# First spectral stage fed with x transposed: mean as a row, rstd behind the product, no transposes

## The chip, the core and the metric

The kernel runs on one core of a Trainium2 chip. The metric is device microseconds of one execution. Three runs of the kernel before gave 1438.41, 1438.85 and 1439.46 us, a median of 1438.85 us.

## The reference

The input x has 2048 rows (positions) of 576 features. Every row is normalised by its mean and variance, and the result goes two ways that are added to x: a filter in the two-dimensional frequency domain, and a gated unit with 4608 hidden features.

```
xn = layernorm(x)                                  # per row of 576, no weights
A  = irfft2(rfft2(xn) * (w_r + 1j * w_i))          # over 2048 x 576
B  = (sigmoid(xn @ w_gate) * (xn @ w_up)) @ w_down # 576 -> 4608 -> 576
out = x + A + B
```

All data are float32.

## The kernel before

Products run on TensorE (PE) in a rounded 32-bit form, and nearly every product is made three times with split operands: a rounded high part (made by ScalarE, ACT) and the rest as a low part (made by VectorE, DVE, as a subtraction). So a value that TensorE is to read passes ACT and then DVE.

The gated unit is the bulk: the rows go in two halves of 1024, and for each half a loop over 36 blocks of 128 hidden features (`unit`) makes seven products (`made(0)` to `made(6)`) of seven matmuls of 512 columns each (tiles `pA`, `pB`, `pE`). In the first half, the weights of a block are split and written to DRAM (`wsp`), and in the second half they come back from there, slice by slice, in one buffer (`w`). After each product of the second half one item of the down projection follows (`seven`, tiles `ps`, six matmuls of 288 columns), whose sums DVE adds to `qs` and `acc`.

The spectral filter runs beside the second half's units, a little after each product, in steps: `active` holds generators, and each `yield` in one is a step, which is one product of seven matmuls and one `ps` item. It has three phases: phase1b (16 tiles of 128 rows, each started 4.1 steps after the last), phase2 and phase3. Phase1b, with rows of 576 features stored as 288 and their mirror image, does for each tile `t`:

- load the rows (`xb`) in natural layout, wait four steps, normalise them (`norm`, line 383), add and subtract the mirrored halves (`eo`, line 468), split the last 32 columns (`rp`, lines 204, 205 and 472);
- two steps later, turn the tile by six transposes on PE (`pf`, lines 478 and 479), and split the result out of PSUM into `fh`, `fl` and `fr` (lines 204, 205 and 484);
- two steps later, multiply by the cosine and sine tables: 14 matmuls into `pd` (line 494). Out of `pd` come four pieces of 64 partitions, each as a high part `ah` by ACT and a low part `al` by DVE (lines 204 and 205, inside `split`);
- two steps later, six matmuls into `pa` (line 506) with a table `am`, whose result goes to DRAM (`sc1`) for phase2.

The mean `mv` and reciprocal deviation `rstd` of the second half's rows are made in the first half by `later_stats`, one tile of rows every fourth unit.

The tiles `ps`, `pf`, `pd` and `pa` all come from one PSUM pool with two slots (`pair`). The order on an engine is not the program's alone: the layer that builds the program moves instructions of one engine past each other where it expects a wait, except those marked `keep_in_program_order`. Each engine then runs its own list in order. DMAs of phase1b are issued from the SP queue, which is in order as well.

Of the kernel before, what the change touches and what calls it, by code (L numbers as in the profile page):

```python
# [9 lines left out]
F32 = mybir.dt.float32  # L10
F32R = mybir.dt.float32r
I32 = mybir.dt.int32
AF = mybir.ActivationFunctionType
OP = mybir.AluOpType
PSUM = bass.MemoryType.PSUM

P = 128
S, D, F = 2048, 576, 4608
KD = D // 2 + 1
NQ = KD + 1  # L20
N1, N2 = 64, 32
NT = S // P
EPS = 1e-5
HD = D // 2
FR = HD + 1 - 2 * P
CW = 512
TPC = CW // P
PAIRS = S // (2 * CW)
TPP = 2 * TPC
KT = 2  # L30
REM = HD - KT * P
# [6 lines left out]
KR = 3 * REM  # L38
# [84 lines left out]
COLS = np.concatenate([np.arange(HD), np.arange(HD, D)[::-1]])  # L123
ROWS = np.arange(S).reshape(N1, N2).T.ravel()


def _layout(x, w_r, w_i, w_gate, w_up, w_down):

    ks = np.concatenate([np.arange(KT * P), np.tile(np.arange(KT * P, HD), 4)])
    w = np.stack([w_gate[COLS], w_up[COLS]]).reshape(2, 2, HD, NF, P)[:, :, ks]  # L130
    w = w[[1, 1, 0, 0], [0, 1, 1, 0]].reshape(4, KT + 1, P, NF, P).transpose(3, 2, 0, 1, 4)
    v = np.stack([w_r, w_i])[:, :, KOF].reshape(2, N1, N2 // 2, 2, KD).transpose(2, 1, 0, 3, 4)
    v = np.broadcast_to(v[:, None], (N2 // 2, 2, N1, 2, 2, KD))
    lay = {"x": x.reshape(S, D)[ROWS][:, COLS].reshape(NT, P, D), "ri": v.reshape(N2 // 2, P, 4 * KD),
           "w": w.reshape(NF, P, 4 * (KT + 1) * P), "wd": w_down[:, COLS].reshape(NF, P, D)}
    return {k: np.ascontiguousarray(a) for k, a in lay.items()}

# [5 lines left out]


@with_exitstack
def spectral_glu_kernel(ctx: ExitStack, tc: tile.TileContext, x, ri, w_in, w_down, out):
    nc = tc.nc
    con = {k: nc.inline_tensor(v, name=f"c_{k}").ap() for k, v in _constants().items()}

    def f32(ap):  # L150
        return ap.bitcast(F32)

    def load_r(dst, src):
        nc.sync.dma_start(f32(dst), src)
# [3 lines left out]
    def pair(name):  # L158
        return ps.tile([P, 2, 512], F32, tag="pp", name=name, bufs=2)

    fix = ctx.enter_context(tc.tile_pool(name="fix", bufs=1))
    idf = fix.tile([P, P], F32, name="idf")
    idr = fix.tile([P, P], F32R, name="idr")
    mv = fix.tile([P, NT, 2], F32, name="mv")
    rstd = fix.tile([P, NT], F32, name="rstd")
# [12 lines left out]
    acc = {}  # L178


    sc1 = tc.dram_tile([N2 * P, NQ], F32, name="sc1")
    sc2 = tc.dram_tile([N2 * P, NQ], F32, name="sc2")
    spill = tc.dram_tile([TPP * P, D], F32, name="spill")
# [19 lines left out]
    def split(hi, lo, src, eng=None):  # L203
        nc.scalar.activation(hi, src, AF.Copy)
        (eng or nc.vector).tensor_tensor(lo, src, f32(hi), op=OP.subtract)


    R = {}
# [134 lines left out]
    def load_x(dst, t):  # L343
        nc.sync.dma_start(dst, x[t])
# [7 lines left out]
    def moments(src, t, pool):  # L352
        st = pool.tile([P, 2, 6], F32, tag="st", name=f"st{t}", bufs=2)
        for i in range(2):
            placed(nc.vector.bn_stats(st[:, i, :], src[:, i * HD:(i + 1) * HD]))
        nc.vector.bn_aggr(mv[:, t, :], st.rearrange("p a b -> p (a b)"))

    def scales(t0, n, pool, table):
        ts = slice(t0, t0 + n)
        rs = pool.tile([P, 4, n], F32, tag="rs", name=f"rs{t0}", bufs=2)  # L360
        ve, r0, w0, w1 = (rs[:, i] for i in range(4))
        nc.vector.tensor_scalar(ve, mv[:, ts, 1], EPS, None, op0=OP.add)
        if table:
            nc.scalar.activation(w0, ve, AF.Sqrt)
            nc.vector.reciprocal(r0, w0)
            steps = 1
        else:

            nc.vector.tensor_scalar(w1.bitcast(I32), ve.bitcast(I32), 1, None, op0=OP.logical_shift_right)
            nc.vector.tensor_scalar(r0.bitcast(I32), w1.bitcast(I32), -1.0, float(0x5F3759DF), op0=OP.mult, op1=OP.add)  # L370
            steps = 3
        nc.vector.tensor_scalar(ve, ve, -0.5, None, op0=OP.mult)
        for k in range(steps):
            nc.vector.tensor_tensor(w0, r0, r0, op=OP.mult)
            nc.vector.tensor_tensor(w0, w0, ve, op=OP.mult)
            o = rstd[:, ts] if k == steps - 1 else r0
            nc.vector.scalar_tensor_tensor(o, w0, 1.5, r0, op0=OP.add, op1=OP.mult)
        nc.vector.scalar_tensor_tensor(nmr[:, ts], mv[:, ts, 0], -1.0, rstd[:, ts], op0=OP.mult, op1=OP.mult)

    def norm(o, a, t):  # L380

        tc.keep_in_program_order(
            nc.vector.tensor_scalar(o, a, mv[:, t, 0:1], rstd[:, t:t + 1], op0=OP.subtract, op1=OP.mult))

    XS, XR, RM = {}, {}, {}

    def new_xs(p, m):
# [64 lines left out]

    def phase1b(t):
        pool, cf = R["pool"], R["cf"]
        xb = pool.tile([P, D], F32, tag="xb", name=f"xb{t}", bufs=2)
        load_x(xb, t)
        yield
        yield  # L460
        yield
        yield
        norm(xb, xb, t)
        am = pool.tile([P, 2, 2, P], F32R, tag="am", name=f"am{t}", bufs=2)
        load_r(am, con["am"][:, t * 4 * P:(t + 1) * 4 * P].rearrange("p (a h m) -> p a h m", a=2, h=2))
        eo = pool.tile([P, 2, HD], F32, tag="eo", name=f"eo{t}")
        for e, op in ((0, OP.add), (1, OP.subtract)):
            nc.vector.tensor_tensor(eo[:, e], xb[:, :HD], xb[:, HD:], op=op)
        rp = pool.tile([P, 2, 3, REM], F32R, tag="rp", name=f"rp{t}")
        rem = eo[:, :, 2 * P:]  # L470
        split(rp[:, :, 0, :], rp[:, :, 1, :], rem)
        nc.scalar.activation(rp[:, :, 2, :], rem, AF.Copy)
        yield
        yield
        pt = pair(f"pf{t}")
        for e in range(2):
            for k in range(2):
                nc.tensor.transpose(pt[:, 0, (2 * e + k) * P:(2 * e + k + 1) * P], eo[:, e, k * P:(k + 1) * P], idf)  # L478
            nc.tensor.transpose(pt[:KR, 1, e * P:(e + 1) * P].bitcast(F32R), rp[:, e].rearrange("p a b -> p (a b)"), idr)
        fh = pool.tile([P, 2, 2, P], F32R, tag="fh", name=f"fh{t}")  # L480
        fl = pool.tile([P, 2, 2, P], F32R, tag="fl", name=f"fl{t}")
        fr = pool.tile([P, 2, P], F32R, tag="fr", name=f"fr{t}")
        split(fh, fl, pt[:, 0, :].rearrange("p (e k s) -> p e k s", e=2, k=2))
        nc.scalar.activation(fr[:KR], pt[:KR, 1, :2 * P].rearrange("p (e s) -> p e s", e=2), AF.Copy)
        yield
        yield
        pd = pair(f"pd{t}")
        for e in range(2):
            steps = []
            for k in range(2):  # L490
                steps += [(fh[:, e, k, :], cf[:, e, k, :]), (fl[:, e, k, :], cf[:, e, k, :]), (fh[:, e, k, :], cf[:, e, 2 + k, :])]
            steps.append((fr[:KR, e, :], cf[:KR, e, 4, :]))
            for n, (l, r) in enumerate(steps):
                nc.tensor.matmul(pd[:, e, :NQ], l, r, start=n == 0, stop=n == len(steps) - 1)  # L494
        ah = pool.tile([P, 2, NQ], F32R, tag="ah", name=f"ah{t}", bufs=1)
        al = pool.tile([P, 2, NQ], F32R, tag="al", name=f"al{t}", bufs=1)
        for sl in range(2):
            for ci in range(2):
                o = slice(ci * N1, (ci + 1) * N1)
                split(ah[o, sl, :], al[o, sl, :], pd[sl * N1:(sl + 1) * N1, ci, :NQ])  # L500
        yield
        yield
        pa = pair(f"pa{t}")
        for sl in range(2):
            for n, (h, m) in enumerate(((0, ah), (0, al), (1, ah))):
                nc.tensor.matmul(pa[:, sl, :NQ], am[:, sl, h, :], m[:, sl, :], start=n == 0, stop=n == 2)  # L506
        x1 = pool.tile([P, 2, NQ], F32, tag="x1", name=f"x1{t}", bufs=1)
        nc.scalar.activation(x1, pa[:, :, :NQ], AF.Copy)
        nc.sync.dma_start(sc1[2 * t * P:(2 * t + 2) * P].rearrange("(j p) n -> p j n", j=2), x1)
# [422 lines left out]
    def later_stats(t):  # L932
        xt = R["pool"].tile([P, 5, HD], F32, tag="xa", name=f"xt{t}", bufs=TPC)
        xt = xt.rearrange("p a d -> p (a d)")[:, :D]
        load_x(xt, t)
        for _ in range(4):
            yield
        moments(xt, t, R["pool"])
        if t == NT - 1:
            scales(TPP, TPP, R["pool"], False)  # L940

    def blocks(p, c):
        for mm in range(2):
# [76 lines left out]
    for p in range(PAIRS):  # L1020
# [38 lines left out]
        for f in range(G, NF):  # L1059
# [16 lines left out]
            if p == 0 and f and f % 4 == 0:  # L1076
                sides.append(later_stats(TPP + f // 4 - 1))
# [62 lines left out]
```

## Time and profile before

| what | value |
|---|---|
| median of three runs | 1438.85 us |
| the profiled execution, whole | 1438.32 us |
| its span, first to last instruction | 1436.5 us |
| PE busy | 1422.8 us (99%) |
| DVE busy | 1087.7 us (76%) |
| ACT busy | 653.5 us (45%) |
| DMA queue q1, share of 16 engines | 69.8% |
| phase1b in the span | from about 736 us (first `pf`) to 954 us (last `pa`) |

The span is the time between the first and the last instruction; the whole execution has 1.8 us more around it. PE is nearly always busy by the profile, but matmuls overlap in flight, so the busy time and the single durations of PE say less than the distance from one piece of work to the next. The chain of waits (the page's part 4) gives that distance.

### The profile page before, as it was taken

Reading aid. Unit: us, or ns where it says so; the run is one execution under the profiler, and the core shown is the slowest. Engines: PE = TensorE matmul, PEld = TensorE weight load, DVE = VectorE, ACT = ScalarE, POOL = GpSimd, SP = SyncE. Lnnn points to the kernel's source line nnn. Section 1 sums busy time; section 2 is a strip of 40 time slices with the busy share of each in tenths; the row PEclk is TensorE's granted clock in tenths of the full one; section 3 lists DMA queues with packets and bytes.
Section 4 is the critical chain, followed back from the end, with each engine's and each line's share of the span. In section 5 each row is a group of like instructions: output and inputs, shape, how many; then the busy total and the mean of one; then the engine's idle time right before and its main releaser. Section 6 shows DMA issues by size and latency. Waiting matters only on the chain.

```text
span 1436.5 us, 21196 instructions
## 1 busy us (share of the span) xinstructions
PE 1422.8 (99%) x8073; PEld 1252.0 (87%) x8073; DVE 1087.7 (76%) x1734; ACT 653.5 (45%) x1122; POOL 3.3 (0%) x5
## 2 busy tenths in 40 slices
PE   8999999999999999999999999999999999999998
PEld 5888888888888888889888888888888889898997
DVE  7988888888888787766366687767888877766784
ACT  6644444444444444453345454434555534443431
POOL 0000000000000000000000000000000000000000
PEclk9999999999999999999999999999999999999999
DMA  7588677776777776655676766778888787776642
GB/s 247 195 329 313 256 274 264 265 264 255 262 255 271 262 276 232 230 215 181 213 215 204 210 201 207 206 220 269 273 270 269 245 282 243 226 227 195 202 125 83
DMA packets 128325, 338.79 MB, mean 236 GB/s; under 512 B 11872, under 2 KB 49248, under 8 KB 123360
## 3 DMA queue, kind: packets, MB, share of 16 engines
q1 hardware_dynamic: 127296, 336.13, 69.8%
q8 instruction: 64, 1.05, 0.3%
q10 hardware_dynamic: 928, 1.31, 0.2%
q14 instruction: 37, 0.30, 0.1%
HBM read 201.27 MB, written 136.12 MB: 235 GB/s over the span
## 4 chain that ended last, share of the span: by engine, by line
PE 97%; DVE 1%; ACT 1%; issue 0%; DMA 0%; ACTq 0%
PE pB L644 24%; PE po L751 19%; PE pE L644 16%; PE pA L644 16%; PE ps L842 12%; PE pe L602 2%; PE pd L494 2%; PE pc L546 1%; PE pa L506 1%; PE pb L530 1%; PE py L573 1%; PE pf L478 1%; PE pz L585 1%; PE b L900 0%; PE px_S L442 0%; PE px_A L442 0%
## 5 line engine op out<-in xcount | busy, mean ns | idle before, releaser
L644 PE MATMUL pB<-X,w 128*128 128x512 f32 x1484 | 382.4, 394 | 0.0
L644 PEld LDWEIGHTS pB<-X,w 128*128 128x128 f32 x1484 | 267.5, 188 | 49.5 <-ACT v L708 1.3
L644 PE MATMUL pE<-X,w 128*128 128x512 f32 x1064 | 273.1, 393 | 0.0
L644 PE MATMUL pA<-X,w 128*128 128x512 f32 x1008 | 259.7, 394 | 1.9 <-DVE X L448 1.2
L644 PEld LDWEIGHTS pE<-X,w 128*128 128x128 f32 x1064 | 192.8, 188 | 34.0
L644 PEld LDWEIGHTS pA<-X,w 128*128 128x128 f32 x1008 | 184.2, 189 | 35.8 <-DVE X L448 1.9
L751 PE MATMUL po<-wd,hh 128*128 128x288 f32 x1216 | 210.9, 295 | 0.0
L842 PEld LDWEIGHTS ps<-wf,hs 128*128 128x128 f32 x1260 | 188.6, 188 | 19.3 <-DVE qs L852 1.8
L842 PE MATMUL ps<-wf,hs 128*128 128x288 f32 x1260 | 204.2, 296 | 0.3 <-DVE qs L852 0.3
L751 PEld LDWEIGHTS po<-wd,hh 128*128 128x128 f32 x1216 | 184.4, 188 | 11.2
L755 DVE TENSOR_TENSOR acc<-acc,po 128x576 f32<-128x576 f32 x168 | 126.0, 750 | 76.7 <-PE po L751 75.5
L236 ACT ACTIVATE w<-raw 128x768 fp32r<-128x768 f32 (+1 forms) x106 | 100.8, 952 | 94.2 <-PE pE L644 37.9
L751 PE MATMUL po<-wd,hl 128*128 128x288 f32 x608 | 128.9, 293 | 0.0
L852 DVE TENSOR_TENSOR qs<-qs,ps 128x576 f32<-128x576 f32 x112 | 84.1, 751 | 31.1 <-PE ps L842 30.0
L751 PEld LDWEIGHTS po<-wd,hl 128*128 128x128 f32 x608 | 98.7, 189 | 0.0
L852 DVE TENSOR_TENSOR acc<-acc,ps 128x576 f32<-128x576 f32 x90 | 67.5, 750 | 24.2 <-PE ps L842 23.6
L238 DVE TENSOR_TENSOR w<-raw,w 128x512 fp32r<-128x512 f32 (+1 forms) x106 | 81.9, 773 | 3.2 <-ACT w L236 2.9
L729 DVE TENSOR_TENSOR y<-y,g 128x1024 f32<-128x1024 f32 x67 | 81.9, 1222 | 3.2
L709 DVE TENSOR_TENSOR y<-v,pE 128x512 f32<-128x512 f32 x68 | 46.7, 686 | 49.1 <-ACT v L708 48.2
L778 ACT ACTIVATE hs<-y 128x512 fp32r<-128x512 f32 x105 | 64.9, 629 | 38.9 <-DVE y L729 12.4
L712 ACT ACTIVATE g<-pB 128x512 f32<-128x512 f32 x68 | 40.7, 598 | 91.1 <-PE pB L644 91.1
L708 ACT ACTIVATE v<-pB 128x512 f32<-128x512 f32 x68 | 40.7, 598 | 71.9 <-PE pB L644 71.5
(165 smaller groups left out, 1667.9 us busy)
## 6 DMA issues: line engine op xcount, KB each, us to landing
w<-wsp SPq DMA_DIRECT2D x246, 320.0 KB, 3.5
wsp<-w SPq DMA_DIRECT2D x34, 2240.0 KB, 7.8
raw<-in_w SPq DMA_DIRECT2D x34, 768.0 KB, 9.7
wdsp<-wd SPq DMA_DIRECT2D x36, 576.0 KB, 4.6
wf<-tsp SPq DMA_DIRECT2D x60, 288.0 KB, 3.8
wf<-wdsp SPq DMA_DIRECT2D x45, 288.0 KB, 4.0
std<-in_wd SPq DMA_DIRECT2D x36, 288.0 KB, 5.4
ri<-in_ri SPq DMA_DIRECT2D x16, 578.0 KB, 5.3
```

The costliest lines, as they stand in the source:

```text
L236: placed(nc.scalar.activation(o[:, :, :3, :], src, AF.Copy))
L238: placed(nc.vector.tensor_tensor(o[:, :, 3:, :], src[:, :, :KT, :], f32(o[:, :, :KT, :]), op=OP.subtract))
L644: nc.tensor.matmul(bank, w[:, sw, :], X[:, x, sx, :], start=start and j == 0, stop=stop and j == len(STEPS) - 1, skip_group_check=skip)
L708: nc.scalar.activation(v[:, 1], bank["B"], AF.Copy)
L709: nc.vector.tensor_tensor(y[:, 1], v[:, 1], bank["E"], op=OP.add)
L712: nc.scalar.activation(g[:, 1], bank["B"], AF.Sigmoid)
L729: nc.vector.tensor_tensor(y, y, g, op=OP.mult)
L751: nc.tensor.matmul(pd[:, b, :HD], h[i], w[k][b], start=g == 0 and n == 0, stop=g == G - 1 and n == 2)
L755: nc.vector.tensor_tensor(a, a, pd[:, :, :HD], op=OP.add)
L778: nc.scalar.activation(hs[:, 0], src, AF.Copy)
L842: nc.tensor.matmul(pd[:, i, :HD], h[:, a, m], w[:, b], start=q == 0, stop=q == 2)
L852: nc.vector.tensor_tensor(o, o, pd[:, :, :HD], op=OP.add)
```

## The change

The rows for phase1b are handed over a second time, as a second input `xt`, already transposed: partitions are features, columns are the tile's 128 rows, and both mirrored halves stand side by side. The 32 remaining features of a half are written four times over, so that a third block of 128 partitions holds their copies. Everything between the load and `pd` then works in that layout, and PE makes no `pf`.

The mean is no longer a value per partition but a row. Subtracting the halves cancels it, so only the sum needs it, as twice the mean, from a tile `mb` on which the row of means has been spread over the partitions by a DMA. The rows come from two new transposes (`prow`) at the end of `later_stats`, through a DRAM tile `rowd`. The factor `rstd` is applied behind the product, where rows are partitions again: ACT scales by it as it makes `ah`, and DVE's subtraction for `al` becomes a three-operand instruction that multiplies by it first. The number of matmuls in `pd` and `pa` stays. The two steps between `eo` and `pf` fall away, and the load of `am` is issued at the tile's start instead of four steps later.

```diff
 def phase1b(t):
-        xb = pool.tile([P, D], F32, tag="xb", name=f"xb{t}", bufs=2)
-        load_x(xb, t)
+        xs = pool.tile([P, 2, KT + 1, P], F32, tag="xs", name=f"xs{t}", bufs=2)
+        nc.sync.dma_start(xs.rearrange("p h k s -> p (h k s)"), xt[t])
+        mb = pool.tile([P, P], F32, tag="mb", name=f"mb{t}", bufs=2)
+        nc.sync.dma_start(mb, rowd[0, t].partition_broadcast(P))
+        am = pool.tile([P, 2, 2, P], F32R, tag="am", name=f"am{t}", bufs=2)
+        load_r(am, con["am"][...])
         yield   # four times
-        norm(xb, xb, t)
-        am = pool.tile(...); load_r(am, con["am"][...])
-        eo = pool.tile([P, 2, HD], F32, tag="eo", name=f"eo{t}")
-        for e, op in ((0, OP.add), (1, OP.subtract)):
-            nc.vector.tensor_tensor(eo[:, e], xb[:, :HD], xb[:, HD:], op=op)
-        rp = pool.tile([P, 2, 3, REM], F32R, tag="rp", name=f"rp{t}")
-        rem = eo[:, :, 2 * P:]
-        split(rp[:, :, 0, :], rp[:, :, 1, :], rem)
-        nc.scalar.activation(rp[:, :, 2, :], rem, AF.Copy)
-        yield
-        yield
-        pt = pair(f"pf{t}")
-        for e in range(2):
-            for k in range(2):
-                nc.tensor.transpose(pt[:, 0, ...], eo[:, e, k * P:(k + 1) * P], idf)
-            nc.tensor.transpose(pt[:KR, 1, ...].bitcast(F32R), rp[:, e]..., idr)
-        split(fh, fl, pt[:, 0, :].rearrange("p (e k s) -> p e k s", e=2, k=2))
-        nc.scalar.activation(fr[:KR], pt[:KR, 1, :2 * P]..., AF.Copy)
+        eo = pool.tile([P, 2, KT + 1, P], F32, tag="eo", name=f"eo{t}")
+        tc.keep_in_program_order(nc.vector.tensor_tensor(eo[:, 1], xs[:, 0], xs[:, 1], op=OP.subtract))
+        nc.vector.scalar_tensor_tensor(xs[:, 0], mb.unsqueeze(1).to_broadcast([P, KT + 1, P]), -2.0, xs[:, 0], op0=OP.mult, op1=OP.add)
+        nc.vector.tensor_tensor(eo[:, 0], xs[:, 0], xs[:, 1], op=OP.add)
+        nc.scalar.activation(fh, eo, AF.Copy)
+        nc.vector.tensor_tensor(fl, eo[:, :, :KT], f32(fh[:, :, :KT]), op=OP.subtract)
+        r = slice(REM, 2 * REM)
+        nc.vector.tensor_tensor(fh[r, :, KT], eo[r, :, KT], f32(fh[r, :, KT]), op=OP.subtract)
         yield
         yield
...
-                split(ah[o, sl, :], al[o, sl, :], pd[sl * N1:(sl + 1) * N1, ci, :NQ])
+                v, r = pd[i, ci, :NQ], rstd[i, t:t + 1]
+                nc.scalar.activation(ah[o, sl, :], v, AF.Copy, scale=r)
+                nc.vector.scalar_tensor_tensor(al[o, sl, :], v, r, f32(ah[o, sl, :]), op0=OP.mult, op1=OP.subtract)
...
 # later_stats, behind the last tile's scales:
+            yield
+            pr = pair("prow")
+            rows = R["pool"].tile([NT, 2, P], F32, tag="xa", name="rows", bufs=TPC)
+            for i, v in enumerate((mv[:, :, 0], rstd)):
+                nc.tensor.transpose(pr[:NT, i, :P], v, idf)
+            nc.scalar.activation(rows, pr[:NT, :, :P], AF.Copy)
+            nc.sync.dma_start(rowd.rearrange("i t p -> t i p"), rows)
```

Since nine lines come in ahead of it and some go, line 494 (`pd`) of before is 482 in the changed kernel, 506 (`pa`) is 497, 644 is 635 and 842 is 833.

The order moves with it, and only between 736 us and the end of phase1b; elsewhere it differs by the two `prow` alone. On PE, the second tile of phase1b stood so before, from its transposes to the first of its `pd`:

```order
L644 MATMUL pB_6649<-X,w_6208 128x512 x4
L478 MATMUL pf_6813<-idf,eo_6753 128x128 x2
L644 MATMUL pB_6649<-X,w_6208 128x512 x2
L842 MATMUL ps_2_1_6834<-wf_2_6668,hs_2_6721 128x288
L479 MATMUL pf_6813<-idr,rp_6756 96x128
L478 MATMUL pf_6813<-idf,eo_6753 128x128 x2
L479 MATMUL pf_6813<-idr,rp_6756 96x128
L842 MATMUL ps_2_1_6834<-wf_2_6668,hs_2_6721 128x288 x5
L644 MATMUL pE_6650<-X,w_6208 128x512 x7
L842 MATMUL ps_3_0_6851<-wf_3_6719,hs_3_6799 128x288 x6
L494 MATMUL pd_6865<-cf,fh_6820 128x290
L494 MATMUL pd_6865<-cf,fl_6821 128x290
```

The same place on PE in the changed kernel, up to the first `pd` that reads the low part:

```order
L635 MATMUL pB_6663<-X,w_6215 128x512 x7
L833 MATMUL ps_2_0_6803<-wf_2_6682,hs_2_6747 128x288 x6
L482 MATMUL pd_6817<-cf,fh_6765 128x290
L635 MATMUL pB_6663<-X,w_6215 128x512 x3
L482 MATMUL pd_6817<-cf,fl_6766 128x290
```

The transposes are gone, `pd` stands about two steps earlier, and three matmuls of `pB` have been moved in between its first matmul (which reads `fh`) and its second (which reads `fl`). Ten of the 16 tiles have such a piece of 2 to 4 matmuls there; before, none had.

On PE again, from the last `pd` of the third tile to its first `pa`, before:

```order
L494 MATMUL pd_7012<-cf,fr_6968 128x290
L644 MATMUL pB_6906<-X,w_6208 128x512 x7
L842 MATMUL ps_5_1_7058<-wf_5_6858,hs_5_6945 128x288 x6
L644 MATMUL pB_6906<-X,w_6208 128x512 x7
L842 MATMUL ps_6_0_7076<-wf_6_6942,hs_6_7008 128x288 x6
L506 MATMUL pa_7089<-ah_7027,am_6891 128x290
```

And in the changed kernel:

```order
L482 MATMUL pd_6953<-cf,fh_6895 128x290 x2
L635 MATMUL pB_6910<-X,w_6215 128x512 x7
L833 MATMUL ps_4_1_6986<-wf_4_6810,hs_4_6877 128x288 x6
L635 MATMUL pA_6909<-X,w_6215 128x512 x7
L833 MATMUL ps_5_0_7004<-wf_5_6874,hs_5_6949 128x288 x6
L635 MATMUL pB_6910<-X,w_6215 128x512 x4
L497 MATMUL pa_7018<-ah_6968,am_6774 128x290
```

The work between `pd` and the `pa` that needs its split result has grown by four matmuls of 512 columns. Over all 16 tiles there stand 12 `ps` matmuls in between, before and after, and beside them before 15, 15, 14, 15, 15, 14, 14, 17, 14, 15, 14, 14, 14, 19, 14, 12 matmuls of 512 columns (235 in all), and now 20, 15, 18, 15, 15, 13, 16, 20, 17, 12, 17, 17, 15, 17, 20, 16 (263).

On DVE, the third tile's preparation stood so before:

```order
L383 TENSOR_SCALAR xb_6760<-xb_6760,mv,rstd 128x576
L468 TENSOR_TENSOR eo_6893<-xb_6760 128x288 x2
L205 TENSOR_TENSOR rp_6896<-eo_6893,rp_6896 128x2x32
L205 TENSOR_TENSOR fl_6967<-pf_6959,fh_6966 128x512
L205 TENSOR_TENSOR al_7028<-pd_7012,ah_7027 64x290 x2
```

And in the changed kernel, where `L843` is the addition of a `ps` item and the `al` are the second tile's:

```order
L464 TENSOR_TENSOR eo_6891<-xs_6770 128x384
L465 SCALAR_TENSOR_TENSOR xs_6770<-mb_6772,xs_6770 128x384
L491 SCALAR_TENSOR_TENSOR al_6833<-pd_6817,rstd,ah_6832 64x290
L466 TENSOR_TENSOR eo_6891<-xs_6770 128x384
L843 TENSOR_TENSOR acc<-acc,ps_2_1_6850 128x2x288
L491 SCALAR_TENSOR_TENSOR al_6833<-pd_6817,rstd,ah_6832 64x290
L470 TENSOR_TENSOR fl_6896<-eo_6891,fh_6895 128x512
L472 TENSOR_TENSOR fh_6895<-eo_6891,fh_6895 32x2x128
L491 SCALAR_TENSOR_TENSOR al_6833<-pd_6817,rstd,ah_6832 64x290
```

One tile's preparation now lies between another tile's `al`, where before the two followed each other.

More of the change, by code (lines that the diff above doesn't have):

```diff
@@ L133, in _layout @@
     v = np.broadcast_to(v[:, None], (N2 // 2, 2, N1, 2, 2, KD))
-    lay = {"x": x.reshape(S, D)[ROWS][:, COLS].reshape(NT, P, D), "ri": v.reshape(N2 // 2, P, 4 * KD),
+    x = x.reshape(S, D)[ROWS][:, COLS]
+    xt = x.reshape(NT, P, 2, HD)[..., ks].reshape(NT, P, 2, KT + 1, P).transpose(0, 4, 2, 3, 1)
+    lay = {"x": x.reshape(NT, P, D), "xt": xt.reshape(NT, P, 2 * (KT + 1) * P), "ri": v.reshape(N2 // 2, P, 4 * KD),
            "w": w.reshape(NF, P, 4 * (KT + 1) * P), "wd": w_down[:, COLS].reshape(NF, P, D)}
@@ L145, in spectral_glu_kernel @@
 @with_exitstack
-def spectral_glu_kernel(ctx: ExitStack, tc: tile.TileContext, x, ri, w_in, w_down, out):
+def spectral_glu_kernel(ctx: ExitStack, tc: tile.TileContext, x, xt, ri, w_in, w_down, out):
     nc = tc.nc
@@ L178, in spectral_glu_kernel @@
     acc = {}
+    rowd = tc.dram_tile([2, NT, P], F32, name="rowd")
     sc1 = tc.dram_tile([N2 * P, NQ], F32, name="sc1")
@@ L378, in scales @@
         nc.vector.scalar_tensor_tensor(nmr[:, ts], mv[:, ts, 0], -1.0, rstd[:, ts], op0=OP.mult, op1=OP.mult)
-    def norm(o, a, t):
-        tc.keep_in_program_order(
-            nc.vector.tensor_scalar(o, a, mv[:, t, 0:1], rstd[:, t:t + 1], op0=OP.subtract, op1=OP.mult))
     XS, XR, RM = {}, {}, {}
@@ L456, in phase1b @@
         pool, cf = R["pool"], R["cf"]
-        xb = pool.tile([P, D], F32, tag="xb", name=f"xb{t}", bufs=2)
-        load_x(xb, t)
+        xs = pool.tile([P, 2, KT + 1, P], F32, tag="xs", name=f"xs{t}", bufs=2)
[3 more added lines that the diff above has]
+        am = pool.tile([P, 2, 2, P], F32R, tag="am", name=f"am{t}", bufs=2)
+        load_r(am, con["am"][:, t * 4 * P:(t + 1) * 4 * P].rearrange("p (a h m) -> p a h m", a=2, h=2))
         yield
@@ L462, in phase1b @@
         yield
-        norm(xb, xb, t)
-        am = pool.tile([P, 2, 2, P], F32R, tag="am", name=f"am{t}", bufs=2)
-        load_r(am, con["am"][:, t * 4 * P:(t + 1) * 4 * P].rearrange("p (a h m) -> p a h m", a=2, h=2))
-        eo = pool.tile([P, 2, HD], F32, tag="eo", name=f"eo{t}")
-        for e, op in ((0, OP.add), (1, OP.subtract)):
-            nc.vector.tensor_tensor(eo[:, e], xb[:, :HD], xb[:, HD:], op=op)
-        rp = pool.tile([P, 2, 3, REM], F32R, tag="rp", name=f"rp{t}")
-        rem = eo[:, :, 2 * P:]
-        split(rp[:, :, 0, :], rp[:, :, 1, :], rem)
-        nc.scalar.activation(rp[:, :, 2, :], rem, AF.Copy)
-        yield
-        yield
-        pt = pair(f"pf{t}")
-        for e in range(2):
-            for k in range(2):
[L478 to L482, printed above, removed]
-        split(fh, fl, pt[:, 0, :].rearrange("p (e k s) -> p e k s", e=2, k=2))
-        nc.scalar.activation(fr[:KR], pt[:KR, 1, :2 * P].rearrange("p (e s) -> p e s", e=2), AF.Copy)
+        eo = pool.tile([P, 2, KT + 1, P], F32, tag="eo", name=f"eo{t}")
+        tc.keep_in_program_order(nc.vector.tensor_tensor(eo[:, 1], xs[:, 0], xs[:, 1], op=OP.subtract))
+        nc.vector.scalar_tensor_tensor(xs[:, 0], mb.unsqueeze(1).to_broadcast([P, KT + 1, P]), -2.0, xs[:, 0], op0=OP.mult, op1=OP.add)
+        nc.vector.tensor_tensor(eo[:, 0], xs[:, 0], xs[:, 1], op=OP.add)
+        fh = pool.tile([P, 2, KT + 1, P], F32R, tag="fh", name=f"fh{t}")
+        fl = pool.tile([P, 2, KT, P], F32R, tag="fl", name=f"fl{t}")
+        nc.scalar.activation(fh, eo, AF.Copy)
+        nc.vector.tensor_tensor(fl, eo[:, :, :KT], f32(fh[:, :, :KT]), op=OP.subtract)
+        r = slice(REM, 2 * REM)
+        nc.vector.tensor_tensor(fh[r, :, KT], eo[r, :, KT], f32(fh[r, :, KT]), op=OP.subtract)
         yield
@@ L491, in phase1b @@
                 steps += [(fh[:, e, k, :], cf[:, e, k, :]), (fl[:, e, k, :], cf[:, e, k, :]), (fh[:, e, k, :], cf[:, e, 2 + k, :])]
-            steps.append((fr[:KR, e, :], cf[:KR, e, 4, :]))
+            steps.append((fh[:KR, e, KT, :], cf[:KR, e, 4, :]))
             for n, (l, r) in enumerate(steps):
@@ L499, in phase1b @@
                 o = slice(ci * N1, (ci + 1) * N1)
-                split(ah[o, sl, :], al[o, sl, :], pd[sl * N1:(sl + 1) * N1, ci, :NQ])
+                i = slice(sl * N1, (sl + 1) * N1)
+                v, r = pd[i, ci, :NQ], rstd[i, t:t + 1]
+                nc.scalar.activation(ah[o, sl, :], v, AF.Copy, scale=r)
+                nc.vector.scalar_tensor_tensor(al[o, sl, :], v, r, f32(ah[o, sl, :]), op0=OP.mult, op1=OP.subtract)
         yield
```

## The prediction, made before the changed kernel was run

> **What bounds the kernel now.** I read the page's busy times first, then the chain that ended last, and then the stretch of phase1b alone: its busy times by engine, its chain, and its waits.
>
> ```profile
> span 1436.5 us, 21196 instructions
> PE 1422.8 (99%) x8073; PEld 1252.0 (87%) x8073; DVE 1087.7 (76%) x1734; ACT 653.5 (45%) x1122; POOL 3.3 (0%) x5
> PE 97%; DVE 1%; ACT 1%; issue 0%; DMA 0%; ACTq 0%
> ```
>
> PE is busy 99% of the span and holds 97% of the chain: the end is set by how much work stands in PE's list, and the other engines count only where PE waits for them. Phase1b, by the busy times of its stretch (span, then PE, weight loads, DVE, ACT, granted clock and DMA share):
>
> ```profile
> 736.00:944.00 208.00, 206.82 (x1206) 177.95 (x1204) 155.41 (x271) 104.37 (x223) 0.00 (x0) 1.00 0.69 203
> ```
>
> PE leaves 1.2 us of 208 idle; DVE is busy 75%, ACT 50%, the DMA engines 69%. So here too work taken out of PE's list is time, as long as DVE and ACT hand over their pieces in time. That they do so only just is seen in the waits of PE's weight loads and in one tile's chain (start, length, work):
>
> ```profile
> PEld pa L506 <- DVE al L205: 1.0, 3, 0.5
> ```
>
> ```profile
> 808.26 0.80 PE ps L842 x6
> 809.06 1.90 PE pd L494 x14
> 810.96 1.63 PE pB L644 x7
> ...
> 815.00 0.79 PE ps L842 x6
> 815.79 0.94 PE pa L506 x6
> ```
>
> ```profile
> 811.05 0.41 ACT L204 ACTIVATE ah<-pd 64x290 fp32r<-64x290 f32 x1 [3.31 <-PE pd L494]
> ...
> 813.42 0.76 DVE L852 TENSOR_TENSOR qs<-qs,ps 128x576 f32<-128x576 f32 x1 [0.55 <-PE ps L842]
> 814.21 0.46 DVE L205 TENSOR_TENSOR al<-pd,ah 64x290 fp32r<-64x290 f32 x1
> ...
> 815.14 0.47 DVE L205 TENSOR_TENSOR al<-pd,ah 64x290 fp32r<-64x290 f32 x1 [0.47 <-ACT ah L204]
> ```
>
> After `pd` ends at 810.96, four pairs of `ah` on ACT and `al` on DVE run strictly in turn, from 811.05 to 815.61, and `pa` goes on at 815.79: PE had 4.83 us of other work, and the pairs took about that. In all 16 tiles `pa` waited 1.0 us.
>
> **What goes from PE.** Six transposes in each of 16 tiles. The chain of 735:944 by line, the pieces of one tile, and the transposes' busy time over the stretch (all their overlaps taken together, in four windows):
>
> ```profile
> by line: PE ps L842 23.9%; PE pB L644 20.7%; PE pA L644 13.4%; PE pd L494 12.7%; PE pE L644 12.4%; PE pa L506 6.1%; PE pf L478 4.3%; PE pf L479 1.3%; DVE hs L779 1.3%; DVE qs L852 0.7%; DVE al L205 0.7%; issue 0.6%; ACT hs L778 0.6%; ACT ah
> ```
>
> ```profile
> 804.20 0.11 issue
> 804.31 0.41 PE pf L478 x2
> ...
> 805.55 0.10 PE pf L479
> 805.65 0.24 PE pf L478 x2
> 805.89 0.06 PE pf L479
> ```
>
> ```profile
> sum 208.00, PE 14.48 PEld 9.15 DVE 10.33 ACT 15.23; mean PE 3.62 PEld 2.29 DVE 2.58 ACT 3.81
> ```
>
> On the chain they hold 4.3% + 1.3% of 209 us, 11.7 us; by their busy time at most 14.5 us. The tile shown has 0.81 us, or 0.92 us with the 0.11 us before the first. I take 12.5 us, the chain's share and part of the "issue" (0.6%, 1.3 us) that stands ahead of transposes.
>
> **What comes to PE.** The two `prow` transposes, once, in the first half. By the pieces above (0.24 us for two that follow each other, 0.41 us where the first has to be got going) they cost 0.24 to 0.41 us, and up to 0.6 us with a wait like that 0.11 us for each. I take 0.4 us. Their copy on ACT and the store of 16 KB to DRAM are read only by the second half and lie beside PE's work.
>
> **What changes on DVE and ACT.** Rows of the same or the nearest form (busy us, mean ns, idle before):
>
> ```profile
> L383 DVE TENSOR_SCALAR xb<-xb,mv,rstd 128x576 f32<-128x576 f32 x16 | 9.3, 579 | 0.5
> L468 DVE TENSOR_TENSOR eo<-xb 128x288 f32<-128x288 f32 x32 | 13.1, 452 | 0.1
> L205 DVE TENSOR_TENSOR rp<-eo,rp 128x64 fp32r<-128x64 f32 x16 | 3.5, 222 | 3.1 <-ACT rp L204 3.1
> L205 DVE TENSOR_TENSOR fl<-pf,fh 128x512 fp32r<-128x512 f32 x16 | 11.0, 689 | 9.2 <-ACT fh L204 8.9
> L205 DVE TENSOR_TENSOR al<-pd,ah 64x290 fp32r<-64x290 f32 x64 | 29.3, 458 | 26.7 <-ACT ah L204 25.4
> L263 DVE TENSOR_TENSOR raw<-raw 128x384 f32<-128x384 f32 x34 | 18.9, 556 | 0.7
> L238 DVE TENSOR_TENSOR w<-raw,w 128x512 fp32r<-128x512 f32 x72 | 49.5, 687 | 0.8 <-ACT w L236 0.5
> L240 DVE TENSOR_TENSOR w<-raw,w 32x256 fp32r<-32x256 f32 x72 | 29.9, 416 | 1.3
> ```
>
> ```profile
> L236 ACT ACTIVATE w<-raw 128x768 fp32r<-128x768 f32 x72 | 61.1, 849 | 53.2 <-DVE raw L263 30.9 <-DVE raw L260 22.1
> L204 ACT ACTIVATE ah<-pd 64x290 fp32r<-64x290 f32 x64 | 26.0, 407 | 44.6 <-PE pd L494 25.1 <-DVE al L205 18.9
> L295 ACT ACTIVATE wd<-std 128x576 fp32r<-128x576 f32 x36 | 24.8, 688 | 4.8 <-PE po L751 3.0
> L413 ACT ACTIVATE xa<-xa,nmr,rstd 128x576 f32<-128x576 f32 x8 | 6.5, 857 | 1.5 <-DMA xa<-in_x 1.5
> ```
>
> DVE loses 0.58 + 2 x 0.45 + 0.22 + 0.69 + 4 x 0.46 = 4.23 us a tile and gets 3 x 0.56 + 0.69 + 0.42 + 4 `al`, 4.60 us at the old price of an `al`. ACT loses three small ones, and its `fh` grows to the 849 ns of the 768-column row. Against 52 us of idle DVE time in the stretch, 0.4 us a tile (6 us) is no bound by itself.
>
> The price that matters is that of a factor per partition, since it lies in the chain from `pd` to `pa`. Before shows it on ACT alone: line 413 with a factor and an offset per partition takes 857 ns where line 295, of the same size and without, takes 688, so 169 ns for two and the function, at the ends 0 or 169 ns for one; I take half, 84 ns. By the Trainium skill ("ScalarE: Activation LUTs", section "What ACT_TABLE_LOAD costs") each operand that is read per partition adds about 93 ns, which fits the half; with 93 for 84, the 16 tiles' pairs would be 0.6 us longer in all. For DVE's three-operand form with such a factor no row exists; I take ACT's 84 ns and ACT's ends. A pair becomes 0.17 us longer (0 to 0.34), four pairs 0.67 us (0 to 1.35).
>
> PE now has 12 `ps` (0.80 us for six) and a mean of 263/16 = 16.4 big matmuls (1.63 us for seven, 0.23 each) between `pd` and `pa`, against 14.7 before. If each tile's pairs took what those shown took, 4.83 + 0.67 = 5.50 us, the place for `pa` would be behind 17 matmuls, and the tiles with fewer (15 four times, 13, 16 twice, 12) would wait 0.46 each, 0.92, 0.23 each and 1.15: 4.4 us in all. A tile without the 0.76 us of line 852 among its pairs needs 4.74 us, and only the ones with 13 and 12 wait, 0.5 us in all. I take the middle, 2.5 us.
>
> In ten tiles `pd` now begins before its low part is ready, with 2 to 4 matmuls, 0.46 to 0.92 us, moved in to cover one `fl` of 0.69 us. What is left I put at 0.5 us (0 to 3 us, if DVE came 0.3 us late in each).
>
> **DMAs.** Each tile loads 384 KB instead of 288, and 64 KB of spread means:
>
> ```profile
> xb<-in_x SPq DMA_DIRECT2D x16, 288.0 KB, 5.1
> ```
>
> ```profile
> SPq L154 <- PE pa L506: 18.8, 14, 2.6
> ```
>
> A load lands 5.1 us after its issue and has four steps, some 9.7 us (4 x 2.43). 2.6 MB more in all is 6% of what moves in the stretch at 203 GB/s, and DMA stands at 0.69. The load of `am`, though issued earlier in the program, waited for the `pa` of two tiles before already, at most 2.6 us, with `w` and `wf` loads queued behind it; none of PE's waits names a DMA there. I cost it at nothing; the slack of those loads covers it, and without that it would be some tenths a tile.
>
> **The sum**, against the profiled execution's 1438.3 us: - 12.5 + 0.4 + 2.5 + 0.5 = 1429.2. The median of the runs lies 0.5 us above that execution, so 1429.7. Its ends: 1438.8 - 14.5 + 0.3 = 1424.6, and 1438.8 - 11.7 + 0.6 + 4.4 + 3.0 = 1435.1.
>
> **Rivals.** *The pairs eat it up.* If a factor costs 169 ns on both engines, the pairs need 4.83 + 1.35 = 6.18 us, the place for `pa` is behind 20 matmuls, and (16 x 20 - 263) x 0.23 = 13 us of waiting come instead of 2.5: 1440, no change. For it speaks that PE came just in time already; against it that 169 ns would mean that line 413's offset is free. Chance 0.10.
>
> *Slower: the three-operand form runs at half rate.* An `al` has 290 columns at (687 - 458)/222 = 1.03 ns, so 0.30 us more; the pairs then need 5.50 + 1.2 = 6.7 us, 22.2 matmuls, and (16 x 22.2 - 263) x 0.23 = 21.2 us of waiting: 1448. It decides from about 6.1 us on, an `al` of some 0.69 us. Rows of that form exist only at 8 columns:
>
> ```profile
> L375 DVE TENSOR_TENSOR rs<-rs 128x8 f32<-128x8 f32 x3 | 0.5, 168 | 0.1
> L377 DVE SCALAR_TENSOR_TENSOR rs<-rs 128x8 f32<-128x8 f32 x2 | 0.3, 168 | 0.1
> ```
>
> They take the same, which at 8 columns says little on the rate: half rate would be 8 ns. Chance 0.08.
>
> *The transposes' durations add up.* With 64 of 284 ns and 32 of 274 ns, 27 us would go, and the time be 1415:
>
> ```profile
> L478 PE MATMUL pf<-idf,eo 128*128 128x128 f32 x64 | 12.7, 284 | 0.6
> L479 PE MATMUL pf<-idr,rp 128*96 128x128 f32 x32 | 8.6, 274 | 0.1
> ```
>
> Their common busy time of 14.48 us says that they overlap. The Trainium skill ("TensorE: Matmul & The Clock Gate", section "Part 4: PE-mode transpose") gives about 275 ns for one in a kernel's context; 96 of these would be 26.4 us. The durations agree with it, the distances do not. Chance 0.02.
>
> **Numbers.** My forecast has 0.80, and its own range, 1424.6 to 1435.1, is the one I give, rounded up to 1436.0, where "no change" begins: 0.2% of 1438.85, 2.9 us, is about what a measurement of this kernel can tell. Faster: 0.80 and 0.02; no change: 0.10; slower: 0.08.
>
> **What would show it.** In the profile after, `pf` is missing, and the stretch of phase1b is shorter by about 10 us. `ah` should last about 0.49 us and `al` about 0.54. Waits of `pa` for `al` should grow from 1.0 to some 2 to 3 us. I am wrong if PE's waits for `al` or `fl` come to over 8 us, if an `al` lasts 0.69 us or more, or if a DMA (`xs`, `mb`, `am`) shows among PE's or DVE's releasers.

## The result

The changed kernel took a median of 1429.07 us in four runs (1427.87 to 1429.69), against 1438.78 us before: a ratio of 0.9931 with a 95% interval of 0.9914 to 0.9948, so 9.7 us less. The forecast was 1429.7 us.

The page of the profiled execution after (1428.53 us), its span and busy times by engine:

```profile
span 1426.7 us, 20983 instructions
PE 1412.8 (99%) x7979; PEld 1243.9 (87%) x7979; DVE 1097.7 (77%) x1734; ACT 651.2 (46%) x1075; POOL 3.3 (0%) x5
```

PE is as busy as before, with 94 instructions less: 96 `pf` gone and two `prow` come. How long the stretch of phase1b takes is best read between two marks on PE that both kernels have, the first `ps` and the first `pb` of phase2. In the tile views, the first number behind the durations is the start of a line's first instruction. Before:

```profile
L842 PE MATMUL ps<-wf,hs x1260: 288/295/402, 735.2 to 1374.4; 128*128 128x288 f32 x180
L530 PE MATMUL pb<-x2h,bmt x64: 294/299/311, 975.4 to 1149.9; 128*128 128x290 f32 x64
```

After:

```profile
L833 PE MATMUL ps<-wf,hs x1260: 288/295/402, 735.6 to 1364.7; 128*128 128x288 f32 x180
L521 PE MATMUL pb<-x2h,bmt x64: 294/298/311, 965.7 to 1140.2; 128*128 128x290 f32 x64
```

The stretch went from 240.2 to 230.1 us, 10.1 us shorter, and from `pb` to the last `ps` both kernels take 399.0 us. So the gain lies in phase1b. I call this distance "the stretch" below; a second profile of the changed kernel gave 230.0 us for it.

In it DVE is busier than before (172.14 of 209 us, 82%, where it was 75%), and PE waits for other things. The busy times of 735:944 after (span, then PE, weight loads, DVE, ACT):

```profile
735.00:944.00 209.00, 207.63 (x1176) 179.72 (x1175) 172.14 (x282) 106.50 (x185) 0.00 (x0) 1.00 0.73 223
```

The waits of PE's weight loads in 735:945 after (in all, times, longest):

```profile
PEld pa L497 <- DVE al L491: 3.7, 8, 0.6
PEld pd L482 <- DVE fl L470: 1.0, 4, 0.3
PEld pd L482 <- ACT fh L469: 0.9, 3, 0.3
...
PEld pa L497 <- ACT qs L841: 0.9, 2, 0.6
...
PEld pa L497 <- ACT ah L490: 0.8, 2, 0.4
```

`pa` waited 1.0 us for `al` before and waits 3.7 us now; the waits for `fl` and `fh` are new. The new forms of the instructions, by line (busy, mean ns, idle before):

```profile
L491 DVE SCALAR_TENSOR_TENSOR al<-pd,rstd,ah 64x290 fp32r<-64x290 f32 x64 | 33.2, 519 | 19.5 <-ACT ah L490 18.2
L464 DVE TENSOR_TENSOR eo<-xs 128x384 f32<-128x384 f32 x16 | 8.9, 554 | 0.2
L465 DVE SCALAR_TENSOR_TENSOR xs<-mb,xs 128x384 f32<-128x384 f32 x16 | 8.9, 554 | 0.2
L490 ACT ACTIVATE ah<-pd,rstd 64x290 fp32r<-64x290 f32 x64 | 31.9, 498 | 46.4 <-PE pd L482 28.9 <-DVE al L491 16.6
```

A factor per partition costs 91 ns on ACT (498 against 407) and 61 ns on DVE (519 against 458). The three-operand form without such a factor, line 465, takes the 554 ns of the two-operand one, so the form by itself costs nothing here. And the two `prow`:

```profile
593.05 0.27 PE L936 MATMUL prow<-idf,mv 128*16 128x128 f32 x1
593.16 0.27 PE L936 MATMUL prow<-idf,rstd 128*16 128x128 f32 x1
593.19 1.87 PE L635 MATMUL pE<-X,w 128*128 128x512 f32 x7
```

They begin at 593.05 and the next product at 593.19, and its seven matmuls then take 1.87 us where the same product took 1.77 us before. So the two cost about 0.2 us. They begin 0.11 us apart, though each lasts 0.27 us.

### The profile page after: what moved, and what is told of

Same layout as the page of the kernel before. It is cut to its first block, busy times and chain, and to the rows that moved or that the text cites. A ratio compares the mean times of both kernels' runs of the same rounds, so it can differ in the third digit from the quotient of the medians.

```text
span 1426.7 us, 20983 instructions
## 1 busy us (share of the span) xinstructions
PE 1412.8 (99%) x7979; PEld 1243.9 (87%) x7979; DVE 1097.7 (77%) x1734; ACT 651.2 (46%) x1075; POOL 3.3 (0%) x5
## 5 line engine op out<-in xcount | busy, mean ns | idle before, releaser
L843 DVE TENSOR_TENSOR qs<-qs,ps 128x576 f32<-128x576 f32 x112 | 84.1, 751 | 28.3 <-PE ps L833 27.5
L843 DVE TENSOR_TENSOR acc<-acc,ps 128x576 f32<-128x576 f32 x90 | 67.6, 751 | 23.2 <-PE ps L833 22.6
```

The source lines that it names most:

```text
L843: nc.vector.tensor_tensor(o, o, pd[:, :, :HD], op=OP.add)
```

## The experiments

Two questions were open. Is the gain really PE's time in the transposes, or that of the steps on DVE and ACT and of the PSUM slot, which went with them? And where do PE's new waits come from? The theory: the kernel's time is PE's work, by the distances between its instructions, plus what PE waits for split pieces; the new waits come from the longer pairs of `ah` and `al`.

**The kernel before, without transposes** (`e1_no_turn`). Everything else of before stays, but the pieces are now made from SBUF (an `fh` takes 618 ns where it took 597).

```diff
-        pt = pair(f"pf{t}")
-        ... six nc.tensor.transpose ...
-        split(fh, fl, pt[:, 0, :].rearrange("p (e k s) -> p e k s", e=2, k=2))
-        nc.scalar.activation(fr[:KR], pt[:KR, 1, :2 * P]..., AF.Copy)
+        split(fh, fl, eo[:, :, :2 * P].rearrange("p e (k s) -> p e k s", k=2))
+        nc.scalar.activation(fr[:KR], eo[:KR, :, :P], AF.Copy)
```

> The kernel before with the six transposes of each tile taken away and nothing else of the change: the high and low parts are made from the unturned rows in SBUF, at the same steps, so the output leaves out the turning. Theory (time is PE's work by its distances, plus what PE waits for pieces from ACT and DVE): 13 to 14 us less than before, 1425 to 1426 us, which is 3 to 4 us less than the changed kernel, since the pairs of ah and al stay as short as before. Rival (the transposes' durations add up): 27 us less, about 1412 us. Rival (the gain is that of the steps on DVE and ACT and of the PSUM slot, PE's work was hidden): like the changed kernel, about 1429 us.

It took 1425.85 us (before beside it: 1438.29; ratio 0.9908, 0.9893 to 0.9923).

```profile
L837 PE MATMUL ps<-wf,hs x1260: 288/294/402, 736.0 to 1361.9; 128*128 128x288 f32 x180
L525 PE MATMUL pb<-x2h,bmt x64: 294/298/311, 962.7 to 1137.2; 128*128 128x290 f32 x64
```

The stretch is 226.7 us, 13.5 us less than before. That is what the theory had (13 to 14 us); durations that add up (27 us) are out. The stretch is 3.4 us shorter than with the whole change: so much the rest of the change costs. This run takes the `pf` out of the PSUM slots too, so by itself it doesn't tell the slot from the transposes.

**The changed kernel with transposes added that nothing reads** (`e4_dummy`).

```diff
+        pt = pair(f"pf{t}")
+        for k in range(6):
+            nc.tensor.transpose(pt[:, k // 4, (k % 4) * P:(k % 4 + 1) * P], idf, idf)
         pd = pair(f"pd{t}")
```

> The changed kernel with six transposes of the identity added in each tile ahead of pd, into a PSUM pair that nothing reads. Theory (PE's distances): about 0.7 to 0.85 us for each tile, less what they cover of waits, so 10 to 13 us more than the changed kernel, 1439 to 1442 us. Rival (transposes are hidden in flight, and the change won by other things): within 3 us of the changed kernel.

It took 1439.3 us (ratio to before 1.0007, 0.9997 to 1.0016), 10.2 us above the changed kernel, though these six have no work on ACT or DVE behind them. Its marks:

```profile
L836 PE MATMUL ps<-wf,hs x1260: 290/295/402, 735.4 to 1375.4; 128*128 128x288 f32 x180
L524 PE MATMUL pb<-x2h,bmt x64: 294/298/311, 976.4 to 1150.9; 128*128 128x290 f32 x64
```

The stretch is 241.0 us, 10.9 us more than in the changed kernel. The added `pf` take a PSUM slot as well, but no wait at a `pf` shows, and the waits of PE's weight loads in the stretch come to 10.5 us, where the changed kernel has 11.4 us. So the added time is not waiting, for a slot or for anything else that the profile shows: it is PE's own, and the rival that the other steps or the slot won most of the time falls. The single durations are those of before:

```profile
L477 PE MATMUL pf<-idf x96: 270/272/273, 736.2 to 941.7; 128*128 128x128 f32 x96
```

96 of 272 ns are 26 us, and they cost 10 to 11, some 0.11 us each: here a transpose's duration is mostly flight that the next one overlaps.

Taking the transposes out won 13.5 us of the stretch, and putting six a tile in cost 10.9. In the kernel before, the weight loads of `pf` also waited, 7.3 us in all:

```profile
PEld pf L478 <- issue: 2.3, 6, 0.5
PEld pf L479 <- ACT rp L472: 1.9, 6, 0.5
...
PEld pf L478 <- ACT x L508: 1.5, 5, 0.3
```

Some of the 13.5 us may be these waits, which went with the transposes; the wait for `x`, which reads `pa`, is one for a PSUM slot. No run separates them. A weight load's wait need not be lost time, since matmuls are still in flight: of PE's matmuls themselves, only one `ps` waited in the stretch before, 0.3 us.

**The factor taken out** (`e2_no_factor`).

```diff
-                nc.scalar.activation(ah[o, sl, :], v, AF.Copy, scale=r)
-                nc.vector.scalar_tensor_tensor(al[o, sl, :], v, r, f32(ah[o, sl, :]), op0=OP.mult, op1=OP.subtract)
+                split(ah[o, sl, :], al[o, sl, :], pd[i, ci, :NQ])
```

> The changed kernel with ah and al made as before, without the factor per partition (the output leaves rstd out in the first stage). Theory (the factor's price in the four pairs is what PE's new waits come from): ah back to 407 ns, al to 458 ns, the pairs' chain from 5.6 us to some 5.0 us, and the time 2 to 3 us less than the changed kernel, 1426 to 1427 us. Rival (the waits come from DVE work of the next tile's preparation that stands between the pairs): the pairs still take over 5.3 us and the time is within 0.7 us of the changed kernel.

It took 1425.69 us (0.9909, 0.9894 to 0.9924), 0.3 us under the theory's range, with a stretch of 227.2 us (its first `ps` at 736.3, first `pb` at 963.5), 2.9 us less than the changed kernel. I call the time from the first `ah` of a tile to the end of its last `al` its chain, read from the timelines of ACT and DVE. Its mean over 16 tiles is 4.90 us, where the changed kernel has 5.60, before had 4.65 and the kernel before without transposes 4.76. The waits of PE's weight loads there:

```profile
PEld pa L495 <- DVE al L208: 2.1, 7, 0.5
...
PEld pd L482 <- DVE fl L470: 0.5, 2, 0.3
```

So of the 3.4 us that the rest of the change costs, the factor is 2.9 us. For the rival, that the next tile's preparation between the pairs makes the waits, at most the small rest is left: 0.5 us of the stretch, and chains of 4.90 against 4.76 us.

**More room for the pieces** (`e6_later_both`, a step more ahead of `pd` and of `pa`; then `e3_later_pa`, with the second of these two alone).

```diff
+        yield
         pd = pair(f"pd{t}")
...
+        yield
         yield
         yield
         pa = pair(f"pa{t}")
```

> The changed kernel with one more step ahead of pd and one more ahead of pa, so that PE has some 2.4 us more of other work before it needs fl and al. Theory (PE's remaining excess of 8 us in the stretch is mostly waiting for these pieces): the waits of pa for al and of pd for fl go, and the time is 4 to 6 us less than the changed kernel, 1423 to 1425 us. Rival (the pieces hold a PSUM slot longer and the wait moves to the ps items, or DVE's total work is the bound): within 1.5 us of the changed kernel, with PE waiting at ps for DVE's additions instead.

> The changed kernel with one more step ahead of pa alone. Theory: with 2.4 us more work in between, pa waits for al no more (3.7 us before), and pd's waits for fl stay: 1.5 to 2.5 us less than the changed kernel, 1426.5 to 1427.5 us. Rival (pd's PSUM slot is held as long as before, and ps, which shares two slots with it, waits for DVE's additions instead): within 1 us of the changed kernel.

With both it took 1427.1 us (0.9916, 0.9900 to 0.9933); with the later `pa` alone, 1426.52 us (0.9914, 0.9901 to 0.9928). The stretches are 227.8 us each. The time of the later `pa` is at the lower end of what the theory had for it, and its waits went the theory's way, though `pa` still waits a little for `al`:

```profile
PEld pd L482 <- DVE fl L470: 1.4, 4, 0.5
...
PEld pa L498 <- DVE al L491: 0.8, 2, 0.5
```

The step ahead of `pd` adds nothing, so the first expectation is missed by 2 us. The waits of the one with both show the rival's part:

```profile
PEld ps L835 <- DVE acc L845: 1.9, 4, 0.9
PEld ps L835 <- DVE qs L845: 1.4, 3, 0.5
PEld pB L637 <- ACT v L701: 1.0, 3, 0.6
PEld pa L499 <- DVE acc L845: 0.7, 2, 0.5
```

With both, `pa` waits for `al` no more, and `ps` waits for DVE's additions instead, 3.3 us where it was 1.2 us.

**The pairs taken apart** (`e8_ah_first`: four `ah`, then four `al`; `e10_ah_first_later_pd`: that, and a step more ahead of `pd`).

```diff
+        for o, sl, i, ci in quarters:
+            nc.scalar.activation(ah[o, sl, :], pd[i, ci, :NQ], AF.Copy, scale=rstd[i, t:t + 1])
+        for o, sl, i, ci in quarters:
+            nc.vector.scalar_tensor_tensor(al[o, sl, :], pd[i, ci, :NQ], rstd[i, t:t + 1], f32(ah[o, sl, :]), op0=OP.mult, op1=OP.subtract)
```

> The changed kernel with the four ah written first in the program and the four al behind them, instead of in pairs; every instruction is the same. In the order ACT then waits for no al between two ah, and DVE for one ah only. Theory (the waits of pa come from four pairs that hand over to each other eight times): the chain from the first ah to the last al falls from 5.6 us to 4.1 to 4.6 us, the waits of pa for al from 3.7 us to under 1 us, and the time is 2 to 3.5 us less than the changed kernel, 1425.5 to 1427 us. Rival (four ah in one piece keep ACT from the other work for 2 us, and four al keep DVE): PE waits at pB or ps instead and the time is within 1 us of the changed kernel, or above it.

> The kernel with the four ah ahead of the four al, and one more step ahead of pd. Theory: besides the waits for al, the 2 us for fl and fh go: 3 to 4.5 us less than the changed kernel, 1424.5 to 1426 us. Rival (the waits move on to the ps items): no better than the one without the added step.

Both expectations were missed. The chain fell to 4.23 us, as the theory had it, and `pa` waits 0.8 us for `al`; yet the time is 1430.83 us (0.9941, 0.9928 to 0.9953), with the later `pd` 1430.1 us (0.9937, 0.9924 to 0.9949). The stretches are 231.5 and 230.8 us, no shorter than with pairs (230.1 and 230.0). One tile of the first, on PE, and on ACT and DVE (start, length, idle before):

```profile
842.96 0.95 PE L831 MATMUL ps<-wf,hs 128*128 128x288 f32 x6
843.75 1.77 PE L633 MATMUL pE<-X,w 128*128 128x512 f32 x7
845.35 0.61 PE L633 MATMUL pA<-X,w 128*128 128x512 f32 x2
846.40 1.04 PE L831 MATMUL ps<-wf,hs 128*128 128x288 f32 x6 [0.43 <-DVE al L489]
```

```profile
842.05 2.04 ACT L487 ACTIVATE ah<-pd,rstd 64x290 fp32r<-64x290 f32 x4 [2.68 <-PE pd L482]
844.13 2.12 DVE L489 SCALAR_TENSOR_TENSOR al<-pd,rstd,ah 64x290 fp32r<-64x290 f32 x4 [1.96 <-ACT ah L487]
846.29 0.76 DVE L841 TENSOR_TENSOR acc<-acc,ps 128x576 f32<-128x576 f32 x1
```

`pd` holds one of the two PSUM slots until its last `al` ends, at 846.25. The other has the `ps` of 842.96, done at 843.9, whose addition stands behind four `al` on DVE and begins at 846.29. So the `ps` that PE has next finds no slot until then. Over the stretch, the waits of PE's matmuls and weight loads show this and one thing more:

```profile
PE ps L831 <- DVE al L489: 2.0, 6, 0.4
PEld pB L633 <- ACT v L697: 2.2, 3, 0.8
```

In pairs, that addition stands between two `al`. The same place in the changed kernel:

```profile
844.15 0.51 DVE L491 SCALAR_TENSOR_TENSOR al<-pd,rstd,ah 64x290 fp32r<-64x290 f32 x1 [0.56 <-ACT ah L490]
844.69 0.76 DVE L843 TENSOR_TENSOR acc<-acc,ps 128x576 f32<-128x576 f32 x1
```

So four by four, the chain is a microsecond shorter, and the other slot comes free later. One step of the expectation didn't come about: DVE did not wait for one `ah` only. The first `al` begins at 844.13, when all four `ah` are done (842.05 + 2.04 = 844.09), and `pd` is held the longer for it; why it waited for all four, the runs don't show. The waits of `pB` for ACT's `v` (0.7 us in the changed kernel) are the other half of the rival, ACT kept from its other work. In the run with the later `pd` they are 0.6 us, its `ps` waited 2.4 us for `al`, and its stretch is nearly as long, so the slot is the larger of the two there; what each of the two costs in time is not shown.

**The deviation as a row too, ahead of the product** (`e9b_rstd_row`).

```diff
+        rb = pool.tile([P, P], F32, tag="rb", name=f"rb{t}", bufs=2)
+        nc.sync.dma_start(rb, rowd[1, t].partition_broadcast(P))
...
+        nc.vector.tensor_tensor(eo, eo, rb.unsqueeze(1).unsqueeze(1).to_broadcast([P, 2, KT + 1, P]), op=OP.mult)
...
+        yield
...
-                nc.scalar.activation(ah[o, sl, :], v, AF.Copy, scale=r)
-                nc.vector.scalar_tensor_tensor(al[o, sl, :], v, r, f32(ah[o, sl, :]), op0=OP.mult, op1=OP.subtract)
+                split(ah[o, sl, :], al[o, sl, :], pd[i, ci, :NQ])
```

> The changed kernel with rstd taken as a row too, ahead of the product: a second spread row (rb), one DVE multiplication of 128x768 on eo, and ah and al without a factor; pd one step later. Theory: the pairs' chain falls to 4.9 us as without the factor, and DVE's added 0.95 us a tile lies ahead of pd, which has a step more: 2 to 3.5 us less than the changed kernel, 1425.5 to 1427 us. Rival (DVE has no room left: it is busy 83% of the stretch and gets 0.95 - 0.24 us a tile more): PE waits for fl or at ps and the time is within 1 us of the changed kernel, or above it.

It took 1429.04 us (0.9930, 0.9917 to 0.9944), which is the rival's number, with a stretch of 229.8 us. The factor's 0.15 us in each pair went, and DVE got 952 ns a tile for the multiplication. DVE is now busy 181.57 of 209 us, 87%:

```profile
PEld pa L499 <- DVE al L208: 3.9, 11, 0.7
PEld ps L835 <- DVE acc L845: 1.9, 6, 0.4
```

`pa` waits for `al` as long as in the changed kernel, with shorter `al`: their chain has 5.17 us, where it had 4.90 without factor and without the multiplication. That they stand behind other work of DVE is the likely reason. The added step ahead of `pd` and the added DMA went along with the multiplication, so no run has it alone; no DMA is among what PE waited for.

**The later `pa` once more, beside the changed kernel** (`e3_again`, `a1_after`).

> The changed kernel once more, beside the one with a later pa: 1428.5 to 1430 us.

> The changed kernel with one more step ahead of pa, once more, for a comparison on one chip. Theory (the stretch was 2.3 us shorter in the profile): 1426 to 1427.5 us, 2 to 3 us under the changed kernel. Rival (the difference was between chips): within 1 us of it.

The later `pa` took 1426.86 us (0.9917, 0.9903 to 0.9930) and the changed kernel 1427.7 us (0.9927, 0.9914 to 0.9941), 0.8 us under its own forecast. The stretches are as before, 227.8 and 230.0 us, so the 2.2 us on PE repeat from profile to profile. The whole times differ by 0.8 us here, which is the rival's number and not the theory's 2 to 3 us, and by 2.6 us between the first runs of each; single runs scatter by about 2 us (1425.6 to 1427.7 against 1427.3 to 1429.7). The later `pa` is probably a little faster than the changed kernel; the runs don't settle by how much.

## Why the prediction was right

- **Transposes: 12.5 us forecast.** Without them alone the medians fell by 12.4 us and the stretch by 13.5 us; six a tile put in with no reader cost 10.2 and 10.9 us. The reading that decided this term was the chain's share (11.7 us) against the durations (27 us). Where it lies between 10.9 and 13.5 us depends on the waits that come and go with the transposes, so that 12.5 us came within a microsecond of the stretch is partly a lucky choice between the chain's 11.7 and the busy time's 14.5 us.
- **`prow`: 0.4 us forecast,** about 0.2 us measured, the lower end of the forecast. Their copy on ACT and the store made PE wait nowhere.
- **The price of a factor.** Forecast 84 ns on both engines, measured 91 ns on ACT and 61 ns on DVE, so 0.15 us a pair for 0.17. The 93 ns of the Trainium skill ("ScalarE: Activation LUTs", section "What ACT_TABLE_LOAD costs") are nearer to ACT's 91 than my half of 169.
- **PE's new waits: 2.5 + 0.5 us forecast,** 3.4 us measured as the difference of the stretches with and without the rest of the change, 2.9 of them the factor's. Counting the matmuls between `pd` and `pa` in the order, and holding them against the pairs' length, gave the right size. That the middle of 0.5 and 4.4 us was so near is in part luck: I gave every tile the same pairs, and in the run the tiles lie between 4.68 and 6.52 us. One step of it was incomplete: I let a pair grow by its price alone, 0.67 us for four. The chain grew by 0.95 us, and without the factor it was still 0.25 us longer than before; another tile's preparation between the pairs is the likely reason. The waits of `pd` were put too low: its weight loads waited 1.9 us for `fl` and `fh`, where I had 0.5 us; what that cost in time, no run shows by itself.
- **DMAs: nothing forecast.** `xs` lands in 5.4 us and `mb` in 5.1 us, and no DMA is among PE's or DVE's releasers in the stretch. By the signs that I gave, one row needs a look: at 713 us, ahead of the stretch, an addition on DVE is said to wait 0.8 us for `am`. The kernel before has the same 0.8 us there, with `xb` named, so it isn't the change's.
- **The rivals.** The three-operand form takes what the two-operand one takes (554 ns for 384 columns in both). The other rival had pairs of 6.2 us from the end of `pd` to `pa`; the mean from the first `ah` to the last `al` is 5.60 us, to which the tile shown in the prediction adds 0.09 and 0.18 us at its ends. Five tiles of 16 did go over 6.2 us, but not all, as that rival had it. The waits for `al`, `fl` and `fh`, 5.6 us in all, stayed under the 8 us that would have refuted the sum.

## What to carry to other kernels

Where one engine holds the chain, take what it loses from the distance between its instructions, not from their durations: six transposes of 272 ns cost 0.7 to 0.8 us together. Then hold every piece that it waits for against the work that the order leaves it in between; here 0.6 us of added price in a chain that was just in time gave back a fifth of the gain. A shorter chain isn't yet a shorter wait: see what shares its buffers, and whose release stands behind it in the queue.

## What the runs showed that I had not expected

The chain of `ah` and `al` got 1.4 us shorter with four `ah` ahead of four `al`, and the kernel no faster: 1430.83 us against 1427.7 and 1429.07 us with pairs, where the intervals of the ratios overlap, and a stretch 1.4 us longer. In part at least that is because of who else waits for one of two PSUM slots. And with DVE 87% busy, `pa` waited for shorter `al` as long as it had for longer ones at 82% (3.9 and 3.7 us).
